# mLSTM cell and feed-forward block on one core: the second chunk's scaling, sums, seams and values' load moved ahead, and one pair of loads of the first chunk

## The chip, the cores and the metric

The kernel runs on one core of a Trainium2 chip. The metric is the device time of one execution in microseconds; 7 executions of the kernel before are at hand, and one execution was recorded by the hardware profiler. The engines are named as in the profile: PE is TensorE's matrix multiply and PEld its weight load, DVE is VectorE, ACT is ScalarE, POOL is GpSimd, SP is SyncE, whose queue issues nearly all transfers.

## The reference

For each of 4 batches and 8 heads, a matrix memory of 40 x 40 is carried over 768 steps; the result is gated, and its 320 columns (8 heads of 40) go through a feed-forward block:

```python
m_new = np.maximum(f_gate[:, :, t] + m, i_gate[:, :, t])
f_stab = np.exp(f_gate[:, :, t] + m - m_new); i_stab = np.exp(i_gate[:, :, t] - m_new)
C = f_stab[..., None, None] * C + i_stab[..., None, None] * np.einsum('bhd,bhe->bhde', vt, kt)
n = f_stab[:, :, None] * n + i_stab[:, :, None] * kt
h_tilde = np.einsum('bhde,bhe->bhd', C, qt)
denom = np.maximum(np.abs(np.einsum('bhd,bhd->bh', n, qt))[:, :, None], 1.0)
y[:, :, t] = (1.0 / (1.0 + np.exp(-o_gate[:, :, t]))) * h_tilde / denom
...
h = x @ w_in                                  # x: 3072 x 320, w_in: 320 x 2048
g = h * (1.0 / (1.0 + np.exp(-1.702 * h)))
out = g @ w_out                               # w_out: 2048 x 320
```

All inputs and the output are float32.

## The kernel before

The 768 steps are cut into 6 chunks of 128 (`w` 0 to 5). Within a chunk the recurrence is worked out with matrix products. `columns` turns the gates' running sums into columns `cols`. `weights` makes the decay weights `wt` of a batch. `scores` multiplies them by the products of keys and queries (DVE L353). `values` multiplies them by the values `v_st` (PE L363, PSUM tile `p_o`) and, from the second chunk on, the carried `state` by the queries (PE L368, `p_i`). A chain of seven DVE instructions for each batch (L383 to L393) then makes `y`, and POOL repeats its last 64 columns (L395), so that `seam` can transpose y in three steps of 128 columns (PE L402) and copy it to `xT` (ACT L403). For the next chunk, `scale_values` and `scale_state` multiply `v_st` and `state` by decays on POOL (L409, L415), `new_states` multiplies keys by scaled values (PE L428, 64 matmuls into two tiles `p_c`), and `carry` adds the result to `state` (DVE L436) and sets the ones of `v_st` (POOL L439).

The feed-forward block of a chunk has two halves. The first raises 320 columns to 2048: `up` in the first chunk, `up_fast` with sums in place of some products from the second on (`w` >= 1). The second half brings them back: `down` in the first chunk (16 blocks, `i` 0 to 15, of four row groups each), `down_fast` later. While the second half of chunk `w` runs, the attention of chunk `w + 1` is worked in between: `attention` returns a list of groups, and after each block whose number is in `stops` the next group is run. The order within every queue is the order of the program's calls, written out by hand; there is no scheduler. Each engine takes its instructions in that order, and waits where the next one's input or buffer is not ready.

The weights arrive as 20 pieces. `fetch(n)` issues the transfers of a piece (SP L166), `convert(n)` turns it into the operand form with two ACT instructions (L228, L229) and four DVE ones (L232 to L237). `load` issues keys, queries, values or output gates of some batches (SP L105): in the first chunk batch by batch, 160 KB each, in a fixed order with the first weights; later 640 KB for all four batches. In the first chunk, ACT's queue holds `convert(0, "A")` ahead of the copies of the third batch's transposed keys and queries (L311) and of the exponentials of its weights (L331).

The PSUM pool `ps_a` has four buffers of one tag, handed out in turn: a tile waits until the one four before it has been read.

For the products of `down_fast`, `weight_sums(0)` and `weight_sums(1)` make differences of output weights (DVE L583, 128 x 1280). They need all of `w_out_sb`, whose last piece, 19, is converted at block 10, and nothing in this chunk reads them.

In `attention(1)` the last groups are, after blocks 10, 12 and 15:

```python
... [(seam, w, 0), (seam, w, 1)],
[(values, w, 2, 3), (scale, w, 2), (scale, w, 3)],
[(seam, w, 2), (seam, w, 3), (new_states, w), (carry, w)]]
```

`last_values` is what the later chunks call in that place: with `states=True`, `values` scales the values before its DVE chain is issued, then issues `new_states`, then scales the state.

Of the kernel before, what the change touches and what calls it, by code (L numbers as in the profile page):

```python
# [34 lines left out]
def kernel(  # L35
# [131 lines left out]


    load_gates(0)
    for what, n in (("kq", 0), ("kq", 1), (load_gates, 1), ("vo", 0), ("vo", 1), (fetch, 0), ("kq", 2), ("kq", 3),  # L170
                    (fetch, 1), ("vo", 2), ("vo", 3), *((fetch, n) for n in range(2, 10))):
        if isinstance(what, str):
            load(0, what, slice(n, n + 1))
        else:
            what(n)
# [137 lines left out]
    def spread(w):  # L313

        for b in range(B):
            x = wt[w, b] = work.tile([L, NP, 2, L], FP, tag="wt", bufs=4, name="wt")
            nc.sync.dma_start(out=x.rearrange("s p i t -> s (p i) t"),
                              in_=m_row[w][b * H:(b + 1) * H, :].unsqueeze(0).to_broadcast([L, H, L]))
# [36 lines left out]
    def values(w, *bs, states=False):  # L355
        po, pi = {}, {}
        for b in bs:
            po[b] = ps_a.tile([L, H, D1], FP, tag="a", name="p_o")
            for p in range(NP):
                for i in range(2):  # L360
                    h = 2 * p + i
                    for t in HALVES:
                        T.matmul(po[b][t, h, :], wt[w, b][:, p, i, t], v_st[:, b * H + h, :], start=True, stop=True)  # L363
        for b in bs if w else ():
            pi[b] = ps_a.tile([L, H, D1], FP, tag="a", name="p_i")
            for p in range(NP):
                for t in HALVES:
                    T.matmul(pi[b][t, 2 * p:2 * p + 2, :].rearrange("p a b -> p (a b)"), qT[w, b][:, p, t],  # L368
                             state[:, b * NP + p].rearrange("p a b -> p (a b)"), start=True, stop=True)
        if states:  # L370
            for b in bs:
                scale_values(w, b)
        if states and w:

            new_states(w)
            for b in bs:
                scale_state(w, b)
        for b in bs:
            u = po[b]
            if w:  # L380
                u = work.tile([L, H, D1], FP, tag="u", name="u")
                g = cols[w][:, BH + b * H:BH + (b + 1) * H].unsqueeze(2).to_broadcast([L, H, D1])
                V.tensor_tensor(out=u, in0=pi[b], in1=g, op=OP.mult)  # L383
                V.tensor_tensor(out=u, in0=po[b], in1=u, op=OP.add)

            den = work.tile([L, H, 1], FP, tag="den", name="den")
            V.tensor_scalar(out=den, in0=u[:, :, D:D1], scalar1=-1.0, scalar2=1.0, op0=OP.mult, op1=OP.max)
            V.tensor_tensor(out=den, in0=u[:, :, D:D1], in1=den, op=OP.max)
            V.reciprocal(out=den, in_=den)
            z = eo[w][:, b * H:(b + 1) * H, :]  # L390
            V.scalar_tensor_tensor(out=z, in0=z, scalar=1.0, in1=u[:, :, 0:D], op0=OP.add, op1=OP.mult)
            y = ys[w, b] = work.tile([L, DM + 64], FP, tag="y", name="y")
            V.scalar_tensor_tensor(out=y[:, 0:DM].rearrange("p (h d) -> p h d", d=D), in0=z, scalar=0.5,  # L393
                                   in1=den.to_broadcast([L, H, D]), op0=OP.mult, op1=OP.mult)
            G.tensor_copy(out=y[:, DM:DM + 64], in_=y[:, DM - 64:DM])  # L395
# [185 lines left out]
    def weight_sums(n):  # L581
        out_, in0, in1 = ((t1, w01, w00), (t2, w11, t1), (t4, w10, t2), (w01, w11, w01))[n]
        V.tensor_tensor(out=out_, in0=in0, in1=in1, op=OP.subtract)  # L583
# [51 lines left out]
    def attention(w):  # L635
        if w > 1:

            return [[(columns, w)], [(weights, w, 0), (weights, w, 1)],
                    [(scores, w, 0), (hidden_sums, w - 1, 1, range(4), 3), (scores, w, 1), (weights, w, 2),
                     (weights, w, 3)],  # L640
                    [(values, w, 0), (values, w, 1), (scores, w, 2), (scores, w, 3)] +
                    [(scale, w, b) for b in (0, 1) if w + 1 < NW],
                    [(seam, w, 0), (seam, w, 1), (last_values, w)], [(carry, w)] if w + 1 < NW else [],
                    [(seam, w, 2)], [(seam, w, 3)]]
        return [[(columns, w)], [(weights, w, 0), (weights, w, 1)], [(scores, w, 0), (scores, w, 1)],
                [(weights, w, 2), (gates_out, w), (values, w, 0, 1), (scale, w, 0), (scale, w, 1)],
                [(weights, w, 3), (scores, w, 2), (scores, w, 3)], [(seam, w, 0), (seam, w, 1)],
                [(values, w, 2, 3), (scale, w, 2), (scale, w, 3)],
                [(seam, w, 2), (seam, w, 3), (new_states, w), (carry, w)]]

    def last_values(w):
        values(w, 2, 3, states=w + 1 < NW)
# [102 lines left out]
    for w in range(NW):  # L755
        more = w + 1 < NW
        for j in range(NF // 2):
            if w == 0 and j == 0:
                for pair_ in range(2):
                    for i, g in enumerate(hidden_of(0, pair_)):  # L760
                        A.activation(out=g, in_=first[pair_][i], func=AF.Gelu_apprx_sigmoid)
                    if pair_ == 0:
                        weights_in(0)
            elif w == 0 and j % 2 == 0:
                weights_in(j // 2)
                up(j, j == 2)
            elif w and j % 4 == 0:
                up_fast(w, j, next_keys if more and j == 0 else None)
            if w == 0 and j == 0:
                load_blocks(1, 0)  # L770
                spread(1)
                load_blocks(1, 1)
            if w == 1 and j == 3:
                weight_sums(3)
            if more:
                if j == (0 if w else 4):
                    load(w + 1, "o")
                if j == 4:
                    if w == 0:
                        fetch(17)  # L780
                    load(w + 1, "v")
                    if w:
                        spread(w + 1)
                if j == (4 if w else 6):
                    load(w + 1, "k")
                if w and j == 3:
                    for b in range(2, 4):
                        transposes(w + 1, b)
            if w and j in (3, 7):
                hidden_sums(w, 0, (j // 4 * 2, j // 4 * 2 + 1), 1, 2)  # L790
                if j == 3:
                    hidden_sums(w, 0, (0, 1), 3, 4)
        side = attention(w + 1) if more else []
        if w == 0:

            blocks = [(lambda b=b, n=n: down(w, b, n)) for ns in ((0, 1), (2,), (3,)) for b in range(B) for n in ns]
            stops = (0, 1, 5, 6, 8, 10, 12, 15)
        else:
            blocks = down_fast(w, 0) + down_fast(w, 1)
            stops = (0, 1, 2, 4, 8, 10, 11, 12)  # L800
        for i, block in enumerate(blocks):
            if w == 0:
                weights_in(4 + i)
                if i == 0:
                    load_gates(2)
                if i == 2:
                    for b in range(B):
                        transposes(1, b, slice(0, 1))
                    first_sums((0, 1))
                    for b in range(B):  # L810
                        transposes(1, b, slice(1, 2))
                if i == 10:
                    load_blocks(2)
            elif w + 2 < NW and i == 0:
                load_gates(w + 2)
                load_blocks(w + 2)
            block()
            if i in stops and side:
                run(side.pop(0))
            if w == 1 and i == 1:  # L820
                weight_sums(2)
            if w:
                for at, c, *what in ((0, 0, (2, 3), 3), (1, 0, (2, 3), 4), (1, 1, range(4), 1),
                                     (5, 1, range(2), 2), (6, 1, range(2, 4), 2), (7, 1, range(4), 4)):
                    if i == at:
                        hidden_sums(w, c, *what)
                if i == 2 and not more:
                    hidden_sums(w, 1, range(4), 3)
            elif i in (12, 14):
                weight_sums(i // 2 - 6)  # L830


# [28 lines left out]
```

## Time and profile before

| | |
|---|---|
| median of 7 executions | 488.8 us (487.57 to 490.59) |
| profiled execution, its own time | 488.54 us |
| span of the profiled execution, first to last instruction | 486.8 us |
| TensorE clock granted over the span | 1.00 |
| PE busy / DVE / ACT / POOL, share of the span | 98% / 70% / 45% / 13% |
| first chunk's attention begins / its second feed-forward half begins | 5.2 / 65.6 us |
| second chunk's up_fast begins | 116.9 us |
| transfers | 44.87 MB, of them 43.55 MB on SP's queue |

A row of the timeline gives start, duration, engine, line of the kernel, operation, output and inputs, and how many instructions were merged; in brackets stands how long the engine was idle before it and what ended that. A row of the list of waits gives who waited for whom, the sum in us, how often, and the longest. The time of an execution lies 1.7 us above its span. All times on the timeline count from the first instruction.

### The profile page before, as it was taken

How to read it: one execution, taken by the hardware profiler on the slowest of the kernel's cores; microseconds unless marked ns; L12 is line 12 of the kernel's file. 1: busy time of each engine (PE TensorE's matmuls, PEld its weight loads, DVE VectorE, ACT ScalarE, POOL GpSimd, SP SyncE). 2: the span in 40 equal slices, each digit the busy share in tenths (PEclk: the TensorE clock that was granted, in tenths of full speed). 3: DMA queues.
4: the chain of work that ended last, by engine and by line, in shares of the span. 5: the costliest groups of instructions: out<-in, count | busy, mean ns of one | idle time of the engine just before them, and what ended most of it. 6: DMA issues, size and time to landing. Idle time of an engine off the chain costs nothing. (4 is left out here: it accounts for less than half of the span.)

```text
span 486.8 us, 10443 instructions
## 1 busy us (share of the span) xinstructions
PE 478.7 (98%) x4076; PEld 396.2 (81%) x4076; DVE 342.0 (70%) x855; ACT 221.0 (45%) x575; POOL 64.5 (13%) x103
## 2 busy tenths in 40 slices
PE   8999999999999999999999999999999999999997
PEld 5874456777778999787999877999977999977997
DVE  8788879759978965667776686696576786254831
ACT  6757766402559401466700465900364920255300
POOL 4030002404000330000332000232000120000000
PEclk9999999999999999999999999999999999999999
DMA  9999789863896200996100796200393000000000
GB/s 128 183 276 331 126 163 230 125 73 69 138 225 66 22 28 25 153 210 73 18 29 3 119 253 74 31 28 3 73 263 29 1 10 21 28 1 0 1 27 28
DMA packets 175953, 44.87 MB, mean 92 GB/s; under 512 B 164352, under 2 KB 169504, under 8 KB 175904
## 3 DMA queue, kind: packets, MB, share of 16 engines
q1 hardware_dynamic: 175328, 43.55, 48.0%
q8 instruction: 32, 0.52, 0.5%
q10 hardware_dynamic: 576, 0.66, 0.4%
q14 instruction: 17, 0.14, 0.1%
HBM read 40.17 MB, written 4.01 MB: 91 GB/s over the span
## 5 line engine op out<-in xcount | busy, mean ns | idle before, releaser
L613 PE MATMUL p_out<-w_out_sb,g 128*128 128x160 f32 x480 | 69.8, 301 | 0.0
L403 ACT COPY xT<-p_x 128x384 f32<-128x384 f32 x24 | 10.8, 481 | 128.2 <-PE p_x L402 112.1
L613 PEld LDWEIGHTS p_out<-w_out_sb,g 128*128 128x128 f32 x480 | 66.3, 190 | 1.0
L524 DVE TENSOR_TENSOR g<-p_u,g 128x256 f32<-128x256 f32 x80 | 33.7, 425 | 44.7 <-PE p_u L516 35.0
L521 ACT COPY g<-p_u 128x256 f32<-128x256 f32 x120 | 43.1, 378 | 41.3 <-PE p_u L516 37.1
L528 ACT ACTIVATE g<-g 128x256 f32<-128x256 f32 x120 | 42.4, 426 | 39.1 <-DVE g L524 39.1
L337 POOL TENSOR_SCALAR_AFFINE_SELECT wt<-wt 128x1024 f32<-128x1024 f32 x20 | 23.2, 1162 | 236.9 <-ACT wt L335 187.9
L618 DVE TENSOR_TENSOR o_sb<-o_sb,p_out 128x160 f32<-128x160 f32 x70 | 21.4, 318 | 42.2 <-PE p_out L613 41.8
L335 ACT ACTIVATE wt<-wt,cols 128x128 f32<-128x128 f32 x160 | 47.8, 392 | 0.0
L516 PE MATMUL p_u<-xT,w_in_sb 128*128 128x256 f32 x160 | 38.9, 382 | 0.0
L516 PE MATMUL p_u<-xs,big 128*128 128x256 f32 x160 | 37.9, 380 | 0.0
L544 PE MATMUL p_v<-xT,w_in_x 64*128 64x512 f32 x80 | 37.0, 602 | 0.0
L544 PE MATMUL p_u<-xT,w_in_x 64*128 64x512 f32 x80 | 37.0, 602 | 0.0
L353 DVE TENSOR_TENSOR wt<-p_s,wt 128x512 f32<-128x512 f32 x48 | 30.4, 683 | 9.0 <-POOL wt L337 6.7
L564 PE MATMUL p_out<-w_out_sb,g 128*128 128x320 f32 x128 | 36.1, 436 | 0.0
L613 PE MATMUL p_out<-t,big 128*128 128x160 f32 x240 | 35.5, 301 | 0.0
L516 PEld LDWEIGHTS p_u<-xT,w_in_sb 128*128 128x128 f32 x160 | 29.6, 190 | 5.4 <-DVE o_sb L618 1.5
L516 PEld LDWEIGHTS p_u<-xs,big 128*128 128x128 f32 x160 | 30.0, 190 | 4.6 <-ACT g L521 0.5
L613 PEld LDWEIGHTS p_out<-t,big 128*128 128x128 f32 x240 | 33.3, 190 | 0.2
L564 PEld LDWEIGHTS p_out<-w_out_sb,g 128*128 128x128 f32 x128 | 23.8, 190 | 9.9 <-issue 0.5
L524 DVE TENSOR_TENSOR g<-p_v,g 128x256 f32<-128x256 f32 x80 | 29.9, 415 | 0.0
L544 PEld LDWEIGHTS p_v<-xT,w_in_x 64*128 64x128 f32 x80 | 14.2, 186 | 17.4 <-issue 17.4
(168 smaller groups left out, 862.2 us busy)
## 6 DMA issues: line engine op xcount, KB each, us to landing
wt<-m_row SPq DMA_DIRECT2D x20, 512.0 KB, 6.9
eo<-in_o_gate_dram SPq DMA_DIRECT2D x5, 640.0 KB, 5.6
v_st<-in_v_dram SPq DMA_DIRECT2D x5, 640.0 KB, 8.9
k_st<-in_k_dram SPq DMA_DIRECT2D x5, 640.0 KB, 11.4
out_dram<-o_sb SPq DMA_DIRECT2D x20, 160.0 KB, 1.8
big<-in_moe_w_in_dram SPq DMA_DIRECT2D x5, 512.0 KB, 6.2
k_bl<-in_k_dram SPq DMA_DIRECT2D x40, 64.0 KB, 2.8
q_bl<-in_q_dram SPq DMA_DIRECT2D x40, 64.0 KB, 2.8
```

The lines of the kernel that those rows point to most:

```text
L335: A.activation(out=x[:, h, :], in_=x[:, h, :], func=AF.Exp, scale=-1.0, bias=cols[w][:, b * H + h:b * H + h + 1])
L337: G.affine_select(out=x, in_=x, compare_op=OP.is_ge, fill=0.0, base=0, pattern=[[0, H], [1, L]], channel_multiplier=-1)
L353: V.tensor_tensor(out=wt[w, b][:, :, i, :], in0=pw[i], in1=wt[w, b][:, :, i, :], op=OP.mult)
L403: A.copy(out=xT[w][:, :, b, :], in_=px)
L516: T.matmul(p[k][:, ts[t]], a[:, k // 2, k % 2 * 128:(k % 2 + 1) * 128], b, start=first, stop=True, skip_group_check=True)
L521: A.copy(out=g[k][i][:, ts[t]], in_=chain[k][:, ts[0]])
L524: V.tensor_tensor(out=g[k][i][:, ts[t]], in0=p[k][:, ts[pt]], in1=g[k][i][:, ts[t]], op=OP.add)
L528: A.activation(out=dst, in_=dst if src is None else src, func=AF.Gelu_apprx_sigmoid)
L544: T.matmul(p[k], w_in_x[r, k, :], x[r, 2, :], start=False, stop=True, skip_group_check=True)
L564: T.matmul(po, gs[w, f // 2][:, f % 2, b * L:(b + 1) * L], w_out_sb[:, f, :], start=(f == 0), stop=(f == NF - 1))
L613: T.matmul(po, a(f), b[:, f, :], start=(f == 0), stop=(f == NH - 1))
L618: V.tensor_tensor(out=dst, in0=x, in1=po, op=OP.add)
```

## The change

Six edits, all in the first chunk's program (`w == 0`), which holds the second chunk's attention:

1. The order of the first loads: keys and queries of the third batch are issued before piece 0 of the weights.
2. The second chunk's values are issued where its output gates were (before piece 17), and the gates after piece 17.
3. The last values of the second chunk are made by `last_values`: values of batches 2 and 3 are scaled right after the value and state products, then `state` (a new case for `w == 1`, without `new_states`), and only then is the DVE chain issued, with POOL's copies of y behind the scaling.
4. The seam of batches 2 and 3 follows block 14 instead of block 15.
5. `new_states` and `carry` have a group of their own, after block 15.
6. `weight_sums(0)` and `(1)` are issued after block 11 instead of after blocks 12 and 14.

```diff
     load_gates(0)
-    for what, n in (("kq", 0), ("kq", 1), (load_gates, 1), ("vo", 0), ("vo", 1), (fetch, 0), ("kq", 2), ("kq", 3),
+    for what, n in (("kq", 0), ("kq", 1), (load_gates, 1), ("vo", 0), ("vo", 1), ("kq", 2), (fetch, 0), ("kq", 3),
                     (fetch, 1), ("vo", 2), ("vo", 3), *((fetch, n) for n in range(2, 10))):
...
-        if states and w:
+        if states and w == 1:
+            for b in bs:
+                scale_state(w, b)
+        elif states and w:
...
-                [(values, w, 2, 3), (scale, w, 2), (scale, w, 3)],
-                [(seam, w, 2), (seam, w, 3), (new_states, w), (carry, w)]]
+                [(last_values, w)], [(seam, w, 2), (seam, w, 3)], [(new_states, w), (carry, w)]]
...
-                if j == (0 if w else 4):
+                if w and j == 0:
                     load(w + 1, "o")
                 if j == 4:
-                    if w == 0:
-                        fetch(17)
                     load(w + 1, "v")
                     if w:
                         spread(w + 1)
+                    else:
+                        fetch(17)
+                        load(1, "o")
...
-            stops = (0, 1, 5, 6, 8, 10, 12, 15)
+            stops = (0, 1, 5, 6, 8, 10, 12, 14, 15)
...
-            elif i in (12, 14):
-                weight_sums(i // 2 - 6)
+            elif i == 11:
+                weight_sums(0)
+                weight_sums(1)
```

## The prediction

> **What bounds the kernel now.** I read the page's busy table first, then the list of waits for TensorE alone, then the timeline of each queue around those waits.
>
> ```profile
> PE 478.7 (98%) x4076; PEld 396.2 (81%) x4076; DVE 342.0 (70%) x855; ACT 221.0 (45%) x575; POOL 64.5 (13%) x103
> ...
> PE p_o L363 <- DMA v_st<-in_v_dram: 1.2, 1, 1.2
> PE p_c L428 <- POOL v_st L409: 1.1, 1, 1.1
> ...
> PE p_t L308 <- DMA q_bl<-in_q_dram: 0.3, 1, 0.3
> ```
>
> TensorE is busy for 478.7 of 486.8 us, so a change that adds no matrix work and takes none away can only move the 8.1 us in which it idles. The list of its waits names seven above 0.2 us; the three shown are those that the change is near. In the timeline they stand at 16.85 (0.33 us, the third batch's queries), 84.58 (1.18 us, the second chunk's values) and 116.41 (1.09 us, the scaling of the last batch's values on GpSimd). Together: 2.60 us, the most that the change can win here, 0.53% of 488.8. All other work of the changed stages lies beside TensorE.
>
> **Part 1, the second chunk's values.** The SyncE queue shows the two loads that change places:
>
> ```profile
> 72.64 0.43 SPq L105 DMA_DIRECT2D eo<-in_o_gate_dram  x1
> 73.18 4.59 SPq L166 DMA_DIRECT2D big<-in_moe_w_out_dram  x2
> 77.88 0.38 SPq L105 DMA_DIRECT2D v_st<-in_v_dram  x1
> ...
> 84.58 2.10 PE L363 MATMUL p_o<-v_st,wt 128*64 128x41 f32 x64 [1.18 <-DMA v_st<-in_v_dram]
> ...
> 84.26 1.25 ACT L343 ACTIVATE eo<-eo 128x1280 f32<-128x1280 f32 x1
> ```
>
> The values land 6.6 us after 77.88, at 84.48, and TensorE starts at 84.58; it was free at 83.40. Issued at 72.64 they land at 78.9 to 79.2 (6.3 us is what the gates took from that place, 6.6 what the values took from theirs): 4 us early. Next in line for that matmul is VectorE's product of scores and weights, done at 82.73, so nothing takes the wait's place: -1.18 us. Both loads are 640 KB in the same pieces of one row, so the two issues of the weights' piece between them keep their times, and so does ScalarE's conversion of it at 80.78. What becomes late is the output gate: issued at 77.88, it lands at about 84.5 instead of 78.9. ScalarE's tanh (84.26) then starts some 0.3 us later; behind it in that queue waits the conversion at 85.83, which itself idled 0.32 us for its load, so the queue is level again. VectorE reads the tanh at 88.91 - 1.18 = 87.7; it would be late from a landing of 86.4 on, and even then y is needed by TensorE only at 98.67 - 1.18, where POOL's copies end at 92.8. I cost it at nothing. Bounds of part 1: -1.18 and -1.0.
>
> **Part 2, scaling, sums and seams.** GpSimd's and VectorE's queues, as they are and as the next chunk, which already has the new order of scaling, shows them:
>
> ```profile
> 111.60 1.37 POOL L395 COPY y<-y 128x64 f32<-128x64 f32 x1 [2.24 <-DVE y L393]
> 112.94 0.73 POOL L409 TENSOR_TENSOR v_st<-v_st,cols 128x328 f32<-128x328 f32 x1
> 113.64 2.03 POOL L415 TENSOR_TENSOR state<-state,cols 128x328 f32<-128x328 f32 x1
> 115.63 0.73 POOL L409 TENSOR_TENSOR v_st<-v_st,cols 128x328 f32<-128x328 f32 x1
> ...
> 179.83 1.42 POOL L415 TENSOR_TENSOR state<-state,cols 128x328 f32<-128x328 f32 x2
> 180.75 0.53 DVE L387 TENSOR_SCALAR den<-u 128x8 f32<-128x8 f32 x1
> 185.28 0.24 POOL L395 COPY y<-y 128x64 f32<-128x64 f32 x1 [2.30 <-DVE y L393]
> ```
>
> Now four scalings stand behind the two copies of y, which wait for VectorE; the last values are scaled at 116.36 and 16 of the 64 state matmuls wait 1.09 us. Moved ahead of the copies, the four run from the end of the value matmuls on. In the next chunk, whose values start at 176.98, they end at 181.25, 4.3 us on. Laid onto this chunk (values at 103.73) that is 108.0, and the state matmuls come at 114: the wait goes, -1.09.
>
> The two weight sums (1.49 and 1.48 us) move from behind the chain that makes y to before it. VectorE was idle 2.41 us up to 103.84 and 2.11 us up to 106.44; sums and eviction (2.97 + 0.49) from 101.42 on end at 104.9, so the chain still starts at 106.44, when its matmuls are done. This hides the sums. They are also gone from beside POOL, where the copy took 1.37 instead of 0.24 and a scaling 2.03 instead of 0.73.
>
> New is the seam of batches 2 and 3: it moves from behind the last block of matmuls to before it. TensorE gets there one block (2.19 us) sooner: the value and state products end at 106.89, two blocks of 2.19 follow, the third batch's three transposes (0.33) start at 111.26 and the fourth's third one, which reads POOL's copy, is due at 111.81. The chain ends at 111.47 in this trace, but POOL did not work beside it. In the next chunk it does: one small step takes 0.53 instead of 0.17, y is ready 8.23 us after the values' start instead of 7.74, and its copy at 8.54. Laid onto this chunk: 112.27, plus a few hundredths, against 111.81: TensorE waits 0.5 us. Without the collision the copy would end at 111.84, and the wait be under 0.1. I take 0.52, since the next chunk runs the same instructions in the new order. Behind the waiting transpose stand the last block, the state matmuls and the next stage, so the wait counts in full. ScalarE's copies to xT now follow the third of its four output transfers and not the fourth, which only helps. Nor does the move of the state's sums onto VectorE's end of the stage cost more than 0.12 us: they end 1.4 instead of 1.17 us after the state matmuls, and eight steps later (126.85, against a matmul at 127.41) is the first place where VectorE is close to TensorE. I take 0.05. Part 2: -1.09 + 0.52 + 0.05 = -0.52, bounds -1.05 and -0.2.
>
> [...]
>
> **Part 3, the third batch's keys and queries ahead of the first piece of weights.** ScalarE's queue decides:
>
> ```profile
> 14.87 0.69 ACT L228 ACTIVATE w_in_sb<-big 128x512 f32<-128x512 f32 x1 [1.13 <-DMA big<-in_moe_w_in_dram]
> 16.56 0.59 ACT L311 COPY kT<-p_t 128x512 f32<-128x512 f32 x1 [0.43 <-PE p_t L308]
> 17.52 0.59 ACT L311 COPY qT<-p_t 128x512 f32<-128x512 f32 x1 [0.37 <-PE p_t L308]
> 18.18 1.26 ACT L331 ACTIVATE wt<-p_w 128x512 f32<-128x512 f32 x2
> ```
>
> The keys and queries land at 15.76 and 16.70 now and some 2 us earlier then: TensorE's 0.33 us go. But the conversion of the piece stands in ScalarE's queue ahead of the copies of that same batch, and already waits 1.13 us for its load (issued 9.29, landed 5.6 us later at 14.87). With two 160 KB loads ahead it is issued at 10.5 or later. If f is its landing, the queue needs from there 0.57 + 0.57 (conversion), 0.48 + 0.48 (copies) and 1.1 (exponentials), by the spacing that the same operations show from 21.28 to 24.46: their end is f + 3.2, against 19.44 now. Their two PSUM buffers are those of the scores that TensorE starts at 19.40. So f = 16.2 costs nothing, an earlier one wins up to 0.33, a later one loses f - 16.2. From the issue, f = 10.5 + 5.1 to 5.9 (the latencies of the two first pieces and of the queries) = 15.6 to 16.4. From the order of landing: the piece landed 2.8 us after the load ahead of it (12.1), the second piece 2.6 after its one (18.8). Keys and queries land 0.9 us after one another now (14.89, 15.76, 16.70); two such steps behind 12.1 give 13.9, and the piece 16.5 to 16.7. I take the middle, 16.4: +0.2 us. TensorE has no gap from 19.4 to 83.4, so whatever is lost here stays. Bounds -0.33 and +0.6.
>
> [...]
>
> **Sum.** -1.18 - 0.52 + 0.2 = -1.5 us. The profiled execution took 488.54 (486.8 of span and 1.7 around it) and becomes 487.0; it stood 0.3 below the median of 488.8, so the median becomes 487.3. I give 487.2.
>
> **Rivals.** (a) Small win: the piece lands at 16.7 and the seam waits 0.8, so 0.9 to 1.1 us are won: 487.8, within 0.3% (1.47 us, about what a measurement of this kernel can tell from no change). For it speaks the order of landing, against it that the second piece landed in 5.1 us. (b) Everything fits: the piece lands by 15.9 and POOL does not meet the chain: -0.33 - 1.04 - 1.18 = -2.55, 486.2. The 0.53 us row at 180.75 speaks against it. (c) Slower: the piece is served only with the fourth batch's loads, which land at 18.8. ScalarE, and with it TensorE, then loses 18.8 - 16.2 = 2.6 us, against 1.7 won elsewhere: 489.7. It decides from f = 17.9 on; slower by 0.3% would need 19.4. Against it: the second piece, also with two loads right behind it, landed before both. (d) The values land early but TensorE waits for something else there: no row shows a later releaser than 82.73.
>
> **How the numbers follow.** The forecast as reckoned (-1.2 to -2.0) 0.50, (a) 0.25, (b) 0.17, (c) 0.05, (d) 0.03. The forecast's middle lies at the 0.3% bound: a little more than half of it (0.28), all of (b) and 0.03 of (a), through runs that spread over 487.6 to 490.6, make faster 0.48; slower is (c) and 0.02 of the same spread, 0.07; the rest, 0.45, is same. The range runs from (b) less 0.2 to (a) with part 3 at its bound and 0.4 of spread: 486.0 to 488.5.
>
> **What would show it.** No wait for values near 83; no wait in the state matmuls; a new wait of some 0.5 us at the fourth batch's seam, for POOL's copy; ScalarE's first conversion starting at 16.1 to 16.7 and the scores of the third batch within 0.5 us of 19.4. The prediction is wrong if that conversion starts after 17.5, or if the gates' tanh holds TensorE.

## The result and the profile after

The changed kernel took a median of 487.35 us (28 runs, 486.75 to 489.05) beside 489.07 us for the kernel before (70 runs, 487.04 to 493.58): ratio 0.9961, 95% interval 0.9948 to 0.9974, so 1.3 to 2.5 us less. Two later comparisons gave 0.995 (0.9925 to 0.9975) and 0.9969 (0.9949 to 0.9989). The predicted time was 487.2.

The profiled execution of the changed kernel took 488.87 us (span 487.2). It is one of the slowest two of its 28 and 1.5 us above their median; a second and a third profile of the same kernel, of executions of 487.72 and 487.26 us, are used beside it below. The first lines are the busy table of the page and the list of TensorE's waits:

```profile
PE 478.8 (98%) x4076; PEld 396.8 (81%) x4076; DVE 343.4 (70%) x855; ACT 220.7 (45%) x575; POOL 61.5 (13%) x103
...
PE p_w L325 <- ACT kT L311: 2.5, 1, 2.5
...
PE p_t L308 <- DMA q_bl<-in_q_dram: 0.2, 1, 0.2
PE p_o L363 <- DVE wt L353: 0.2, 1, 0.2
```

TensorE's busy time is what it was (478.7 before). The waits for the second chunk's values and for GpSimd's scaling, 1.18 and 1.09 us, are no longer in the list; the 0.2 us for queries that is left belongs to the first batch (at 6.26). At its head stands a wait that was not there: 2.55 us for ScalarE's copy of the keys. GpSimd is busy 3.0 us less (64.5 before). Some 2.5 us of that come from its copy of y (0.24 us instead of 1.37) and its two scalings of the state (1.42 instead of 2.03 + 0.73), which no longer run beside VectorE's sums.

The timelines of the engines' queues in the same execution, at the places that the prediction names:

```profile
11.02 1.43 SPq L166 DMA_DIRECT2D big<-in_moe_w_in_dram  x1
18.43 0.66 ACT L228 ACTIVATE w_in_sb<-big 128x512 f32<-128x512 f32 x1 [4.70 <-DMA big<-in_moe_w_in_dram]
20.17 0.38 PE L325 MATMUL p_w<-xs 128*128 128x512 bf16 x1 [2.55 <-ACT kT L311]
...
73.88 0.38 SPq L105 DMA_DIRECT2D v_st<-in_v_dram  x1
85.50 2.07 PE L363 MATMUL p_o<-v_st,wt 128*64 128x41 f32 x64
...
107.33 0.50 DVE L386 TENSOR_TENSOR u<-p_i,cols 128x328 f32<-128x328 f32 x1 [1.67 <-PE p_i L368]
108.39 0.53 DVE L390 TENSOR_SCALAR den<-u 128x8 f32<-128x8 f32 x1
112.85 0.24 POOL L398 COPY y<-y 128x64 f32<-128x64 f32 x1 [2.23 <-DVE y L396]
112.19 1.28 PE L405 MATMUL p_x<-ident,y 128*128 128x128 f32 x6
115.56 1.43 PE L431 MATMUL p_c<-v_st,k_st 128*40 128x41 f32 x64
...
127.28 1.42 DVE L527 TENSOR_TENSOR g<-p_u,g 128x256 f32<-128x256 f32 x4
127.47 0.69 PE L547 MATMUL p_v<-xT,w_in_x 64*128 64x512 f32 x1
127.75 0.69 PE L547 MATMUL p_u<-xT,w_in_x 64*128 64x512 f32 x1
```

The line numbers shown are three higher than before from line 373 on, here and in every kernel with the new order of scaling. Read from the top: piece 0 of the weights is issued at 11.02 and ScalarE starts on it at 18.43, 7.4 us later (5.6 before); TensorE stops for 2.55 us ahead of the second half of the third batch's weights (`p_w`). The values are issued at 73.88, 4 us sooner than before, and their matmuls (85.50) start without a wait. The VectorE chain starts at 107.33, held by the products `p_i` and not by the sums: VectorE idled 1.67 us ahead of it. Its step of 0.53 us at 108.39, beside GpSimd's scaling of the state (107.47, 1.42), is the collision that the prediction took from the next chunk. The six transposes of the last seam take 1.28 us where they took 0.82: a wait of 0.46. The state matmuls run through. The first products of the rest rows (the last 64 of the 320 columns, `w_in_x`), `p_v` and `p_u`, began together in the kernel before (both at 127.41) and now lie 0.28 apart.

So this execution won 1.18 + 1.09 us of waits and paid 2.55 - 0.33 + 0.46 + 0.28. By these rows it would be 0.7 us slower than the profiled execution before (488.54); it was 0.33 slower. Most executions of the changed kernel are 1.5 us faster than this one, and the runs had to say why.

### The profile page after: what moved, and what is told of

The parts are those of the page before. It is cut to its first block, busy times and chain, and to the rows that moved or that the text cites. A ratio compares the mean times of both kernels' runs of the same rounds, so it can differ in the third digit from the quotient of the medians.

```text
span 487.2 us, 10445 instructions
## 1 busy us (share of the span) xinstructions
PE 478.8 (98%) x4076; PEld 396.8 (81%) x4076; DVE 343.4 (70%) x855; ACT 220.7 (45%) x575; POOL 61.5 (13%) x103
```

## The experiments

Of the twelve kernels, the first five repeat the change or take it apart, three go beyond it, and the last four test the front and the sums. Each list was run on one chip beside the kernel before: 489.31 us there for the first list (33 runs, 487.45 to 493.84), 488.38 for the second (17 runs, 487.28 to 491.58), 488.18 for the third (35 runs, 487.2 to 493.87). Medians are compared within a list. The theory under test: the three parts add up, the first worth more than its profiled wait because that wait varies from run to run, the third a loss because piece 0 lands late ahead of ScalarE's copies. The rivals: the gain comes from the scaling and sums, or the front is neutral and the 2.55 us an accident without a cause in the change.

### First list: the change taken apart

**The full change once more.**

> The changed kernel as it is, a second time, for another recorded execution. Theory A (the first piece of weights lands late only in some executions: in the recorded one at 18.43 us, 7.4 us after its issue, with an instruction transfer of 16 KB on one of the DMA engines): the piece lands between 15.7 and 17 in this one, TensorE's wait at the second half of the third batch's weights is under 1 us instead of 2.55, and the time is 1.5 to 2 us below the kernel before. Theory B (the piece lands late always, and parts 1 and 2 win more than their rows say): the wait of 2 to 3 us is there again, at about the same time as before the change plus 0.3, or the other parts show more than 2.3 us.

Measured: 487.51 us (486.83 to 487.93), ratio 0.995. In the timeline of this profile the piece is there at 16.70 and the stop is short:

```profile
16.70 0.68 ACT L228 ACTIVATE w_in_sb<-big 128x512 f32<-128x512 f32 x1 [2.95 <-DMA big<-in_moe_w_in_dram]
17.84 0.57 ACT L311 COPY kT<-p_t 128x512 f32<-128x512 f32 x1
...
18.45 0.38 PE L325 MATMUL p_w<-xs 128*128 128x512 bf16 x1 [0.81 <-ACT kT L311]
19.87 1.25 PE L351 MATMUL p_s<-qT,kT 40*128 40x128 f32 x16
```

From the piece to TensorE's matmul it is 1.75 us here and 1.74 in the profile above. What differs is the landing. The copy of the keys ends at 18.41 and TensorE goes on at 18.45; the third batch's scores follow at 19.87.

**Without the new order of the first loads** (parts 1 and 2).

```diff
-    ... ("vo", 1), ("kq", 2), (fetch, 0), ("kq", 3),
+    ... ("vo", 1), (fetch, 0), ("kq", 2), ("kq", 3),
```

> The changed kernel with the first loads in their old order (parts 1 and 2 without part 3). Theory A: the recorded execution shows no wait for the values (1.18 us won), none in the state matmuls (1.09 won), one of about 0.46 at the fourth batch's seam and one of about 0.28 where up_fast takes the rest rows; 1.5 us faster than the kernel before, 0.2 us or so from the full change on either side. Theory B: 3.5 to 4 us faster than before, since the late piece is gone as well.

Measured: 486.92 us (486.56 to 487.31), ratio 0.9928 (0.99 to 0.9956). That is 0.59 below the full change of the same list, where 0.2 us or so on either side was expected. The piece is there at 15.00. TensorE waits 0.45 us for the third batch's queries at 17.14, the very wait that the new order was to remove, and the kernel is faster all the same. Third part: a loss of about 0.6 us.

**The new order of the first loads alone** (part 3).

```diff
-    ... ("vo", 1), (fetch, 0), ("kq", 2), ("kq", 3),
+    ... ("vo", 1), ("kq", 2), (fetch, 0), ("kq", 3),
```

> The kernel before with only the third batch's keys and queries ahead of the first piece of weights (part 3 alone). Theory A: between 0.5 us faster and 0.6 us slower than before, by where the piece lands in the execution (16.2 costs nothing); a recorded execution with a late piece stands above the others. Theory B: 2 us slower. If TensorE loses time there, the later wait for the second chunk's values (1.18 us) shrinks by as much, since the values' transfer does not move with TensorE; so up to 1.2 us of a loss would not show in the total.

Measured: 488.51 us (487.16 to 491.79), ratio 0.9975 (0.9944 to 1.0006). Inconclusive for the part's size: the interval holds a gain of 2.7 us and a loss of 0.3, because the values still come late here and their wait scatters over more than the part is worth. The profile is clear: both later waits are as before (1.18 and 1.08 us), and a stop of 0.54 us at the exponentials, with the piece there at 16.41, stands in place of the 0.33 for the queries. The values' wait did not grow or shrink when TensorE came 0.2 us later: their issue moved along with it (78.14 against 77.88).

**The values' load alone** (part 1).

```diff
-                if j == (0 if w else 4):
+                if w and j == 0:
                     load(w + 1, "o")
                 if j == 4:
-                    if w == 0:
-                        fetch(17)
                     load(w + 1, "v")
                     if w:
                         spread(w + 1)
+                    else:
+                        fetch(17)
+                        load(1, "o")
```

> The kernel before with only the second chunk's values issued ahead of the weights' piece and the output gates behind it (part 1 alone). All theories: TensorE's wait of 1.18 us for the values is gone and no other takes its place, 1.0 to 1.2 us faster than before. A rival: the output gates land late and hold VectorE's chain, which shows as a wait of the step that multiplies by the gates, and the win is under 0.6 us.

Measured: 487.52 us (487.3 to 487.83), ratio 0.9949 (0.9925 to 0.9972): 1.8 us below the kernel before, by two loads that change places, where 1.0 to 1.2 were expected. The wait for values is gone, the wait for GpSimd stays. In its timeline:

```profile
112.28 0.82 PE L402 MATMUL p_x<-ident,y 128*128 128x128 f32 x6
115.22 0.51 PE L428 MATMUL p_c<-v_st,k_st 128*40 128x41 f32 x16 [1.08 <-POOL v_st L409]
```

Six transposes in 0.82 us without a wait, then the stop of 1.08 ahead of the last 16 state matmuls: the old order of scaling. Against this kernel, the second part with its early seam is worth 487.52 - 486.92 = 0.60 us. And the scatter changed: 12 runs lie within 0.5 us, where the kernel before spreads over 6.4 us on the same chip. The fastest runs of the kernel before (487.45) are as fast as this one's median.

The clock has a share in that spread. In 16 of the 85 executions of the kernel before in the three lists the mean granted clock is 0.993 to 0.997; these are all the executions above 490.1 us, and in all others it is 0.999 or 1.000. If the clock is 1.00 or 0.50, as in the profile of a kernel below (0.50 from 19.87 to 30.12 us), a mean of 0.996 over 490 us is some 4 us at half clock and one of 0.993 some 7, which lose at most 2.0 and 3.4 us (an estimate from the means). The longest times are thus more than a wait. Of the executions with early values only those of one kernel below, with the first weights later still, show such a clock.

### Second list: part 2 alone, and beyond the change

**Scaling, sums and seams alone** (part 2).

```diff
+        if states and w == 1:
+            for b in bs:
+                scale_state(w, b)
-        if states and w:
+        elif states and w:
...
-                [(values, w, 2, 3), (scale, w, 2), (scale, w, 3)],
-                [(seam, w, 2), (seam, w, 3), (new_states, w), (carry, w)]]
+                [(last_values, w)], [(seam, w, 2), (seam, w, 3)], [(new_states, w), (carry, w)]]
...
-            stops = (0, 1, 5, 6, 8, 10, 12, 15)
+            stops = (0, 1, 5, 6, 8, 10, 12, 14, 15)
...
-            elif i in (12, 14):
-                weight_sums(i // 2 - 6)
+            elif i == 11:
+                weight_sums(0)
+                weight_sums(1)
```

> The kernel before with part 2 alone: scaling, sums, seam and state sums as changed, both loads in their old places. Theory A (the kernel before scatters over 487.4 to 493.8 us because the second chunk's values, issued last of three large transfers, land at different times, and TensorE waits from 0 to some 6 us for them): this kernel still scatters, by 4 us or more above its fastest execution, and is 0.3 to 0.6 us faster by its fastest execution (1.09 won, 0.46 lost at the fourth batch's seam, 0.27 lost where up_fast takes the rest rows). Theory B (the scatter comes from the scaling on POOL or from elsewhere in the stage): its executions lie within 1.5 us of one another.

Measured: 487.7 us (486.39 to 488.5), ratio 0.9984 (0.9969 to 0.9999). By medians the part wins 0.7 us, as in the first list (0.6), and by the fastest executions 0.89 (486.39 against 487.28), more than the expected 0.3 to 0.6. The wait for values is 1.51 us in this record. The scatter of 2.1 us lies between the two expectations (4 or more, 1.5 or less), on a chip on which the kernel before scattered less too (4.3 us), so it supports only weakly that the late values make the scatter.

**Parts 1 and 2, with the fourth batch's seam back behind the last block.**

```diff
-                [(last_values, w)], [(seam, w, 2), (seam, w, 3)], [(new_states, w), (carry, w)]]
+                [(last_values, w)], [(seam, w, 2)], [(seam, w, 3), (new_states, w), (carry, w)]]
```

(and the first loads in the order of the kernel before)

> Parts 1 and 2 without part 3, and with the seam of batch 3 (the fourth) back behind the last block, that of batch 2 left ahead of it. If the chain that makes y, with POOL's copy behind it, is what holds TensorE there, the 0.46 us wait at the fourth batch's transposes goes, y is long there when they come, and nothing else takes its place: 0.4 to 0.5 us less than with both seams ahead (486.9 on the earlier chip). If those 0.46 us only hide a later wait (the 0.27 us where up_fast takes the rest rows), that one grows to 0.5 or more and the total stays.

Measured: 486.37 us (485.83 to 486.58), ratio 0.9959 (0.9946 to 0.9973). The transposes of the two seams now take 0.49 us each, without a wait:

```profile
110.41 0.49 PE L405 MATMUL p_x<-ident,y 128*128 128x128 f32 x3
110.73 2.32 PE L567 MATMUL p_out<-w_out_sb,g 128*128 128x320 f32 x8
112.89 0.49 PE L405 MATMUL p_x<-ident,y 128*128 128x128 f32 x3
```

The block of matmuls between the two seams (2.32 us) covers VectorE's chain and GpSimd's copy. This is the price of moving both seams ahead of that block: 0.46 us, a wait that the change itself brought. It is read from the rows, since no kernel of this list has both seams ahead and the 486.9 of the first list was measured on another chip. The offset of 0.26 us at the rest rows stays (125.22 and 125.48), so the seam is not its cause.

**Piece 0 later still**, behind the fourth batch's keys and queries too.

```diff
-    ... ("vo", 1), ("kq", 2), (fetch, 0), ("kq", 3),
+    ... ("vo", 1), ("kq", 2), ("kq", 3), (fetch, 0),
```

> The full change with the first piece of weights issued one batch later still, behind the fourth batch's keys and queries as well (part 3 at a double dose). If the landing f of the piece sets TensorE's loss through ScalarE's queue (exponentials end at f + 3.2, no loss at f = 16.2), the piece lands at 18 to 18.7 and TensorE's wait ahead of the third batch's second weights is 2.0 to 2.6 us, in every execution: 1.5 to 2 us slower than the full change, 2.1 to 2.6 slower than without part 3, that is about as fast as the kernel before. If only a chance collision made the recorded landing of 18.43 late, and ScalarE's queue has slack, the time stays within 0.5 us of the full change.

Measured: 492.94 us (490.79 to 494.57), ratio 1.0092 (1.0067 to 1.0116): 4.6 us slower than the kernel before beside it, where about the same time was expected, and far more than the piece is later. The timeline, and then the view by stretches (columns: stretch, its length, busy time of PE, PEld, DVE, ACT, POOL with counts, granted TensorE clock, share of the DMA engines, GB/s):

```profile
19.37 0.66 ACT L228 ACTIVATE w_in_sb<-big 128x512 f32<-128x512 f32 x1 [5.63 <-DMA big<-in_moe_w_in_dram]
21.12 0.58 PE L325 MATMUL p_w<-xs 128*128 128x512 bf16 x1 [3.46 <-ACT kT L311]
...
30.20 1.16 PE L351 MATMUL p_s<-qT,kT 40*128 40x128 f32 x16
```

```profile
19.50:20.00 0.50, 0.00 (x0) 0.00 (x0) 0.00 (x0) 0.50 (x2) 0.00 (x0) 0.87 1.30 246
20.00:20.50 0.50, 0.00 (x0) 0.00 (x0) 0.43 (x1) 0.50 (x3) 0.00 (x0) 0.50 0.91 138
...
29.00:30.00 1.00, 1.00 (x10) 0.76 (x7) 0.93 (x3) 0.97 (x2) 0.00 (x0) 0.50 0.95 336
30.00:31.00 1.00, 1.00 (x17) 0.83 (x17) 0.86 (x2) 0.60 (x1) 0.00 (x0) 0.94 1.07 401
```

The landing is 19.37 and the stop 3.46 us, 1.75 us from one to the other again. But TensorE's clock is halved: the mean of 0.87 from 19.50 to 20.00 puts the fall from 1.00 to 0.50 at 19.87, and the mean of 0.94 from 30.00 to 31.00 the return at 30.12. In all six executions of this kernel the mean granted clock is below 1.00 (0.989 to 0.997). The same matmul takes 0.58 instead of 0.38 us. From the stop's end to the fourth batch's scores TensorE needs 30.20 - 21.12 = 9.08 us; the full change in its third profile needs 23.51 - 18.56 = 4.95. So against that execution (487.26; this one took 493.92, 6.66 more) 2.6 us of the loss are the longer stop, and 4.1 us the clock.

**Parts 1 and 2, split seam, and the second batch's transposes of the third chunk behind the sums.**

```diff
         transposes(w + 1, 0)
-        transposes(w + 1, 1)
+        if w != 1:
+            transposes(w + 1, 1)
...
-                    for b in range(2, 4):
+                    for b in range(1 if w == 1 else 2, 4):
```

> As the kernel with the seam split and the old order of the first loads, and the second batch's two transposes of the third chunk moved from VectorE's queue ahead of up_fast's sums to behind them. The 0.27 us by which the sums are late at the rest rows come from VectorE's queue (state sums end 0.2 us later against the state matmuls, 12 instructions ahead of it): with 1.2 us of transposes out of the way the wait is gone, 0.2 to 0.3 us faster than without this move, and 2.3 to 2.7 us faster than the kernel before. Rival: the transposes are then late for the products of the third chunk, which shows as a wait at the scores of that chunk, and nothing is won.

Measured: 486.05 us (485.88 to 486.3), ratio 0.9956 (0.9943 to 0.9969), the lowest median of the study, 2.3 us below the kernel before of its list and 0.3 below the one above. The runs of the two overlap (6 and 5 of them), and medians of different lists can't be compared this closely: by ratio, parts 1 and 2 alone stand at 0.9928. `p_v` and `p_u` start together again:

```profile
124.81 0.69 PE L547 MATMUL p_v<-xT,w_in_x 64*128 64x512 f32 x1
124.82 0.69 PE L547 MATMUL p_u<-xT,w_in_x 64*128 64x512 f32 x1
```

With two transposes (1.3 us of VectorE's time) moved behind them, the sums that free the PSUM buffers are in time. So the 0.26 us at the rest rows is VectorE's lateness there, as the prediction had placed it. The rival's wait at the third chunk's scores is not in the list of TensorE's waits.

### Third list: what holds the front, and the sums

**The full change, a third time.**

> The full change once more, beside the three kernels that follow. Theory A (TensorE's stop ahead of the third batch's exponentials lasts as long as piece 0 is late, because ScalarE's first conversion stands ahead of the keys' copy): median 487.0 to 488.0, scatter at least 1 us, and in the record a stop at the matmul of xs of 0.5 to 2.6 us put down to ScalarE's copy of the keys, equal to the landing of piece 0 less 15.9 us within 0.2. Rival B (the loss of the first part lies elsewhere, for instance in the later pieces): the stop doesn't follow the landing.

Measured: 486.88 us (486.56 to 487.45), ratio 0.9969. The scatter of 0.9 us and the median are just below what was expected (1 us, and 487.0 to 488.0). Landing 16.81, stop 0.91; of the timeline three rows, of which the last two are VectorE's for the third and the fourth batch's scores:

```profile
18.56 0.38 PE L325 MATMUL p_w<-xs 128*128 128x512 bf16 x1 [0.91 <-ACT kT L311]
...
21.24 1.29 DVE L353 TENSOR_TENSOR wt<-p_s,wt 128x512 f32<-128x512 f32 x2 [1.21 <-PE p_s L351]
25.88 1.28 DVE L353 TENSOR_TENSOR wt<-p_s,wt 128x512 f32<-128x512 f32 x2
```

With this, six records, five of kernels with the new order and the last of the kernel with piece 0 later still, give the table for the expectation's rule:

| piece 0 there at (us) | 16.41 | 16.70 | 16.81 | 16.93 | 18.43 | 19.37 |
|---|---|---|---|---|---|---|
| TensorE's stop (us) | 0.54 | 0.81 | 0.91 | 1.02 | 2.55 | 3.46 |
| landing less 15.9 | 0.51 | 0.80 | 0.91 | 1.03 | 2.53 | 3.47 |

The stop is the landing less 15.9, to 0.03 us: the conversion at the head of ScalarE's queue is shown.

**Piece 0's conversion behind the third batch's seams and scores**, on ScalarE and VectorE.

```diff
     values(0, 0)
-    convert(0, "A")
     values(0, 1)
...
     seam(0, 1)
-    convert(0, "V")
     scores(0, 2)
+    convert(0)
```

> The full change with piece 0's conversion put behind the third batch's seams and scores, on ScalarE and on VectorE. Theory A: the stop at the matmul of xs is gone or below 0.15 us; time 0.4 to 1.0 us below the full change of this call, since two parts without the third were 0.59 below it and the 0.45 us wait for queries is gone as well; scatter below 1 us. Rival B: no gain over 0.25 us, because the conversion that runs 2 to 3 us later holds back the fourth batch's copies on ScalarE or the first half of the feed-forward block, which then begins no sooner than in the full change.

Measured: 487.74 us (487.72 to 488.43): 0.9 us slower than the full change beside it, where theory A expected 0.4 to 1.0 us faster. The stop is gone, as expected, and that is worth nothing:

```profile
20.17 1.29 DVE L353 TENSOR_TENSOR wt<-p_s,wt 128x512 f32<-128x512 f32 x2 [2.50 <-PE p_s L351]
...
24.65 1.11 DVE L235 SCALAR_TENSOR_TENSOR w_in_sb<-big,w_in_sb 128x512 uint32<-128x512 uint32 x1
25.90 1.01 DVE L237 CUSTOM_DVE_ANT_0 w_in_sb<-big,w_in_sb 128x1024 uint16<-128x1024 uint16 x1
26.82 1.27 DVE L353 TENSOR_TENSOR wt<-p_s,wt 128x512 f32<-128x512 f32 x2
...
27.76 1.41 PE L363 MATMUL p_o<-v_st,wt 128*64 128x41 f32 x32 [0.83 <-ACT big L229]
```

The third batch's scores reach VectorE 1.07 us sooner (20.17 against 21.24), but the conversions of two pieces now stand between them and the fourth batch's, which come 0.94 us later (26.82 against 25.88) and hold the value matmuls for 0.83 us. The list names ScalarE as the releaser; what ended last is VectorE's row at 26.82. Of the 0.94 us, 0.74 come from the two rows of 1.11 and 1.01 us, which take 0.69 each in the full change; here GpSimd scales values beside them (24.27, 2.09 us). In the full change piece 0's four VectorE rows (17.59 to 20.03) ran ahead of the third batch's scores, in time in which VectorE had nothing else to do. Theory A was right about the cause of the stop and wrong about its price: the stage has a second bound, VectorE, less than 1 us behind.

**The same, with the split seam and the later transposes**: the edits of the kernel above and of the fastest one, together.

> As the kernel before this one in the list, with the fourth batch's seam one group later and the second batch's transposes of the third chunk behind the sums. Theory A: the stops of 0.46 at the fourth batch's seam and of 0.28 at the rest rows go, 0.6 to 0.9 us below the kernel with the conversion behind alone, 485.2 to 486.0 where the full change is 487.5; no TensorE wait over 0.4 us between 5 and 130 us. Rival B: the first part, without its queue fault, is still no gain: not below 485.9.

Measured: 487.04 us (487.02 to 487.1), 0.70 below the kernel ahead of it, as expected for the seam and the rest rows (0.6 to 0.9), which prices the two within one list. The time itself is a miss, for the reason just shown: 0.16 above the full change beside it, and the ratio of 0.9968 (0.9948 to 0.9988) is not below the 0.9956 of the kernel with the lowest median. But its 12 runs lie within 0.08 us, and 11 of 12 of the kernel ahead of it within 0.08 too. These are the two kernels in whose records TensorE, after the first batch, waits for no load, directly or by way of ScalarE's queue. All others scatter by 0.4 to 6.7 us and have such a wait; that the one makes the other is argued from this, not shown.

**The full change with the two sums after blocks 12 and 14**, where they were.

```diff
-            elif i == 11:
-                weight_sums(0)
-                weight_sums(1)
+            elif i in (12, 14):
+                weight_sums(i // 2 - 6)
```

> The full change with the two sums left behind blocks 12 and 14, where they were. Theory A (the sums ahead of the fourth batch's chain on VectorE make the new wait at its seam): the chain begins about 3 us sooner and ends near 109.8, the 0.46 us stop at the seam is gone, 0.3 to 0.6 us below the full change; what waits next is the read of p_out behind the chain, below 0.2 us. Rival B (the sums must be early, or they hold back TensorE): a stop of 0.5 us or more at p_out, or at the rest rows behind the transposes, and time the same as the full change or above it.

Measured: 487.97 us (487.62 to 488.64), 1.1 above the full change beside it, ratio 0.999 (0.997 to 1.0011). Theory A had it 0.3 to 0.6 faster. The chain of VectorE does not start sooner without the sums ahead of it:

```profile
105.83 0.50 DVE L386 TENSOR_TENSOR u<-p_i,cols 128x328 f32<-128x328 f32 x1 [2.11 <-PE p_i L368]
111.14 1.49 DVE L586 TENSOR_TENSOR t<-w_out_sb 128x1280 f32<-128x1280 f32 x1
111.35 1.37 POOL L398 COPY y<-y 128x64 f32<-128x64 f32 x1 [2.23 <-DVE y L396]
...
112.78 0.33 PE L405 MATMUL p_x<-ident,y 128*128 128x128 f32 x1 [1.06 <-POOL y L398]
```

It starts at 105.83 (105.72 in the full change beside it), because it waits for TensorE's `p_i`. The sum then starts at 111.14, right where GpSimd copies the last y, and the copy takes 1.37 us instead of 0.24. TensorE waits 1.06 us at the last transpose; the six transposes take 2.42 us (110.69 to 113.11) against 1.28 in the full change beside it, and the next stage starts 1.24 us later (116.55 against 115.31, of which 0.11 came with the landing of piece 0). So the sums sooner are not only hidden: they are what keeps the early seam's wait at 0.46. The copy starts 0.21 us after the sum and ends (112.72) 0.09 us after the sum's end (112.63): 1.37 us beside a sum of 1.49. In the profile before, the same pair ends at 112.97 and 112.88.

## Why the prediction was right or wrong

**The total.** 487.2 predicted, 487.35 measured, in a range of 486.0 to 488.5. The likeliest case was that which came, but the terms were less right than the sum: two were too small, with opposite signs, and that they nearly cancel is luck. By the first list, in us:

| | predicted | records | medians |
|---|---|---|---|
| part 1, values | -1.18 | -1.18 | -1.8 |
| part 2, scaling, sums, seam | -1.09 + 0.52 + 0.05 | -1.08 + 0.46 + 0.26 | -0.6 |
| part 3, first loads | +0.2 | -0.45 + 0.81 (or 2.55) | +0.6 |

For part 2 the rows make -0.36; the two profiled executions that differ by it alone (487.30 and 486.92) are 0.38 apart, so the rest of the medians' -0.6 may be scatter.

**Part 1** was right in mechanism: the wait goes, nothing takes its place, the later output gates hold nothing on TensorE. Mis-sized is the step "-1.18 us". It prices the wait of one execution. In the 33 runs of that list the kernel before lay at 489.31 in the middle and 487.45 at best; with the values early, 487.52. A kernel whose median sits 1.8 us above its fastest runs, and which loses nearly all of its spread with two loads exchanged, had a wait that varies, and the profiled execution showed 1.18 us of it (1.18 and 1.51 in two other records with late values). How far it varies is argued from these spreads and from the two kernels that wait for no load and hardly scatter; no record shows it, and in the longest executions up to 3.4 us are the halved clock (an estimate from their mean clock of 0.993).

**Part 2.** The wait at the state matmuls goes (1.08); the wait at the fourth batch's seam is 0.46 against the 0.52 worked out from the next chunk; the step of 0.53 us that made the difference between 0.1 and 0.5 is there. It ends at 108.92, together with GpSimd's scaling (108.89), so the collision cost the 0.36 us of the row (0.53 against 0.17). "This hides the sums" held, and the kernel with late sums shows what the prediction had not counted: their place beside GpSimd's copy would have cost 1.1 us more with the early seam. Mis-sized is "I take 0.05" at the rest rows, with its bound of 0.12: the products start 0.22 to 0.28 us apart in eight records with part 2 and the transposes in their old place. In a ninth, the second profile of the full change, it is 0.89, where a load held VectorE's transpose of the third chunk's queries for 0.51 us. The row before:

```profile
126.85 1.42 DVE L524 TENSOR_TENSOR g<-p_u,g 128x256 f32<-128x256 f32 x4
```

It began 10.00 us after the stage's first matmul (116.85) and begins 10.37 after it now (127.28, 116.91), so VectorE is 0.37 us late where the prediction reckoned with 0.23. And the room was smaller than it read. It set the row's start (126.85) against the matmul at 127.41. But `p_u` starts right behind the first of these sums, which takes 0.42 us: in the second profile it ends at 126.58 and `p_u` starts at 126.64. It ended at 127.27 before, just in time, and ends at 127.70 after, and `p_u` starts at 127.75.

**Part 3.** The rule "f = 16.2 costs nothing, a later one loses f - 16.2" held: the stop is f - 15.9, and 0.3 to 0.45 us of other wait is gone. Its path was another, though. The prediction had TensorE wait at the scores, for the exponentials that end at f + 3.2. The runs have it wait earlier, for the copy of the keys, and TensorE's own work from there to the scores takes 1.42 us (18.45 to 19.87 in the second profile), so that they begin at f + 3.17: the two agree by luck. Mis-sized is the step "I take the middle, 16.4" (the two estimates' own middle is 16.3). The order of landing gave 16.5 to 16.7 and the issue 15.6 to 16.4; four of five records of kernels with this order show 16.4 to 16.9, and one 18.43. The issue, too, was taken at 10.5 and is at 11.0, since the two loads ahead of it took 0.85 and 0.92 us to issue. With 11.0 the issue gives 16.1 to 16.9, which fits too. The middle of the five records, 16.81, makes +0.6 by the prediction's own rule, as the medians do. By its own signs the prediction failed in the profile after: the conversion starts at 18.43, behind the 17.5 that it named, and the third batch's scores at 21.58; in the other four records they start at 19.58 to 20.09, two of them within 0.5 us of 19.4.

**The rivals.** (a), the small win, had the right landing but too much for the seam. (b) failed by the seam and the landing. (c) asked for f of 17.9 or more: it happened in one execution of five profiled with that order, and this is why the profile after shows so little gain. Whether the piece then came with the fourth batch's loads, as (c) has it, is open. It had a worse continuation that wasn't seen: in the kernel with piece 0 later still, behind a stop of 3.46 us, TensorE's clock is halved for a while (0.50 from 19.87 to 30.12 us), and the loss more than doubles. (d) did not come: nothing took the place of the wait for values. "No gap from 19.4 to 83.4, so whatever is lost here stays" held for the loss, but the reverse failed in the kernel with the conversion behind: a stop that is removed there need not be won, as VectorE was close behind.

**What stays open.** Why piece 0 came 1.5 to 2 us later in one execution. The shares of the DMA engines in that profile fall to 0.08 in the last half microsecond ahead of its landing, about one of sixteen at work, so the transfers were not short of room. The transfer of instructions that the first expectation suspects begins between 16.2 and 16.4 us in this record, ahead of the landing at 18.43; no run tests it. And the spread of the values' wait, for which no record above 1.51 us exists.

## What to carry to other kernels

Where the runs before spread widely, one profiled wait is a sample: price its removal by the distance from the median to the fastest runs as well, and look at the granted clock of the slowest (0.993 to 0.997 here in the runs of the kernel before above 490.1 us). A load moved ahead of another pays only if what it overtakes isn't converted, on an in-order queue, ahead of the very thing that was to come sooner (here the stop was the landing less 15.9 us, and about 0.6 us were lost); write the break-even as a landing time, and look for the engine that is second before counting the stop as won. And before a seam or a copy is moved up, see which long VectorE instruction would then run beside GpSimd (here a copy of 0.24 us took 1.37 beside a sum of 1.49).

## What the runs showed that was not expected

TensorE's clock. In the kernel with piece 0 later still, after 2.2 us without a matmul (17.65 to 19.87), the granted clock fell from 1.00 to 0.50, and came back at 30.12, 10.25 us later, though TensorE was busy without a gap from 21.12 on: 9.00 us of work without a stop ran at half clock. A stop of 2.55 us in the profile after (17.62 to 20.17) left it at 1.00, so the length of the stop alone doesn't decide. Where the mean clocks of whole executions are below 0.999 they lie at 0.996 to 0.997, 0.993 and 0.989 to 0.990, which is some 3 to 4, 7 and 10 us at half clock (an estimate, for 490 us, with a clock of 1.00 or 0.50 as in this record). What makes the clock fall, and what sets how long it stays there, is not shown.

GpSimd and VectorE slowed each other in both directions: VectorE's small step took 0.53 us instead of 0.17 beside GpSimd's scaling (1.42), and GpSimd's copy of y 1.37 instead of 0.24 beside VectorE's sum (1.49).
